# Routing groups of 8, 8, 8 and 12 tiles, evenly stepped, and two drains of GpSimd before the end, in an attention kernel with a top-1 mixture of experts

## The chip, the cores and the metric

One core of a Trainium2 chip runs the whole program. The time is device microseconds of one execution. The engines are named as in the profile: PE is TensorE (PEld its weight loads), DVE is VectorE, ACT is ScalarE, POOL is GpSimd, SP is SyncE, which here only issues transfers.

## The reference

For each of 8 batches and 8 heads, a 64 by 64 matrix kv is formed from k and v over 576 positions, q is multiplied by it, and the result is normed. The 4608 rows of 512 numbers then go through a mixture of 8 experts: each row goes to the expert with the greatest logit, alone.

```python
kv = np.einsum('bhsd,bhse->bhde', k, v)
out = np.einsum('bhsd,bhde->bhse', q, kv)
rms = np.sqrt(np.mean(out * out, axis=-1, keepdims=True) + 1e-06)
x = rows of (out / rms * g_norm)          # 4608 x 512

logits = x @ w_gate                        # 8 experts
e_idx = np.argmax(logits, axis=1)
gate_w = softmax(logits)[arange(N), e_idx]
eom = 1.0 / (1.0 + np.exp(-(x @ w_output_gate)))
for e in range(E):
    mask = e_idx == e
    h = np.maximum(x[mask] @ w1[e], 0.0)   # 512 -> 1024
    ye = h @ w2[e]                         # 1024 -> 512
    out[mask] = gate_w[mask, None] * eom[mask, e, None] * ye
```

## The kernel before

The kernel has two phases.

**Phase 1, attention and routing.** It goes through the 8 batches. For each, TensorE sums k and v into kv (`kvps`, L495), VectorE copies it (`kvc`, L503), and small matmuls make from it the matrix `aug`, which holds kv and its product with the gate's weights (`kvTps`, `mps`; `cps` at L477 is a filler that only keeps TensorE at work). Then the 36 tiles of 128 rows follow, 4.5 to a batch: `out_tile` multiplies q by `aug` (`ops`, L565), ScalarE copies the rows to `xrow` (L570), squares them (`sq`, L572) and copies the raw products with the gate's weights (`gp`, L573). One tile later VectorE sums the squares (`ss`, L586). Rows go to a table `xs` in memory in pieces of two tiles (`xs<-xrow`, L795, issued by SP), their scales in a second write per group (`xs<-xtail`, also L795).

The routing of the tiles is done in groups. `GR` gives their sizes, here 10, 10, 4 and 12 tiles. When the last tile of a group has its `ss`, a generator `route(gi)` starts for it, and after every further tile `advance` lets it go on to its next pause. How many tiles a pause lasts stands in a table, with 1 where nothing stands:

```python
WAITS = {(0, 2): 3, (1, 7): 2, (1, 2): 0, (1, 8): 2, (1, 5): 0, (0, 8): 2, (0, 6): 2}

def pause(k):
    for _ in range(WAITS.get((gi, k), 1)):
        yield 1
```

`route` computes on VectorE 1/rms (into `xtail`), scales the gate's products with it (`gp`, L642; for group 0 on GpSimd, for groups in `APART` in two halves, the gate's first), sums them to logits (`lg`, L646), finds the expert and writes a one-hot (`ohb`, L672). Matmuls on it (`rps`, L700 to L707) give each row its rank within its expert, `slots` and the remainder `lon`. Out of `lon` comes for each tile a 128 by 128 one-hot `la` (L743); `PLACES` says for each group which engine makes which: V is VectorE, P GpSimd, A ScalarE. With three VectorE operations `rrc` (L753 to L760) and `la`, TensorE sums a table of which row stands at which place of which expert (`tblps`, L773), from which VectorE makes the indices `gidx` and `oidx` of gathers and scatters.

The expert with most of the first 24 tiles is found at the end of the third group (`cnt` to `epos`); SP reads its number (`TENSOR_LOAD`) to choose the weights. Its first 384 rows form the lead run, which starts while the last 12 tiles are still being computed and routed. In both kernels the third group ends with tile 23.

**Phase 2, the experts.** There are nine runs: the lead run, the rest of that expert, and the seven others. Each run is gathered with one indirect DMA for each tile of 128 rows (`gather`, L244, on GpSimd's software queue), scaled by head with 1/rms (`scale_heads`, L252, GpSimd), transposed (`stage`) and multiplied with both weights (`mm1` L314 to `hps`, `mm2` L363 to `yps`). Weights come by SP (`wload`, L199) and are split in two parts (L219 to L229). ScalarE and VectorE scale the result (`y`, L373 or L371), and GpSimd scatters its rows to the output (L374). Run i+1 is gathered while run i is in its `mm1`.

In phase 1 the order is as the code is written, on every engine. In phase 2 it is written out by hand for TensorE, VectorE and ScalarE, and a scheduler sets it for GpSimd and SP. At the end stands a loop over rows that found no room in their expert's places (L1100; with these inputs it runs zero times), and the end of the program (L1168), where every engine drains and meets the others.

Of the kernel before, what the change touches and what calls it, by code (L numbers as in the profile page):

```python
# [21 lines left out]
P = 128  # L22
# [21 lines left out]

NOVER = NT + E

GR = (10, 10, 4, 12)
GROUPS = [list(range(sum(GR[:i]), sum(GR[:i+1]))) for i in range(len(GR))]
GMAX = max(GR)

LEAD_TILES = 24
LEAD_GROUP = [sum(GR[:i + 1]) for i in range(len(GR))].index(LEAD_TILES)
LEAD = LEAD_TILES * P // E // P * P

RUNS = [(0, 0, LEAD), (0, LEAD // P, CAP[0] - LEAD)] + [(p, 0, CAP[p]) for p in range(1, E)]
# [16 lines left out]
HOOKS = {15: 'R', 27: 'RR', 28: 'R', 31: 'RGW', 32: 'X', 34: 'NL'}  # L72
TAIL = "QLLLLRRRSLSRRSLLRRRLSLRRSRLSLL"

WAITS = {(0, 2): 3, (1, 7): 2, (1, 2): 0, (1, 8): 2, (1, 5): 0, (0, 8): 2, (0, 6): 2}

GPSIMD_GROUPS = 1
APART = (2,)


SPLITS = ['VV', 'AV', 'AV', 'AV', 'AV', 'AV', 'AV', 'AV']
NORMS = ("PPP", "VVVV")
PLACES = ['P', 'P', 'PAV', 'VAV']


COLD_B = 3
# [43 lines left out]
def tiles_of(i):  # L130

    _, t0, n = RUNS[i]
    return [(t0 + k, k * P, min(P, n - k * P)) for k in range(-(-n // P))]
# [6 lines left out]
def body(ctx: ExitStack, tc: tile.TileContext, kvm, rem, qT, wg, gn, w1, w2, kc, xs, tab, out):  # L140
    nc = tc.nc
# [39 lines left out]
    def give(t):  # L181
        free.append(held.pop(id(t))[0])
# [56 lines left out]
    def gather(i):  # L239
        p = RUNS[i][0]  # L240
        rows = xs[0:1 + LEAD_TILES * P] if i == 0 else xs
        for t, c0, M in tiles_of(i):
            x = take([P, XW], F32, "xg")
            nc.gpsimd.indirect_dma_start(  # L244
                out=x[:M, :], out_offset=None, in_=rows,
                in_offset=bass.IndirectOffsetOnAxis(ap=gidx[:M, p, t:t + 1], axis=0))
            xg[(p, t)] = x

    def scale_heads(x, eng):
        v = x[:, 0:DM].rearrange("p (h d) -> p h d", d=D)  # L250
# [88 lines left out]
    def mm2(i, k, events):  # L339
        nonlocal ny  # L340
        p = RUNS[i][0]
        t, c0, M = tiles_of(i)[k]
        C = RUNS[i][2]
        T = half(i)
        ps = ps_y.tile([P, DM], F32, name="yps", tag=f"y{ny % 2}")
        ny += 1
        tl = tails.pop((p, t))
        for f in range(8):
            h = h_of(i, f)
            wh, wl = wgt[(2, f // 2)]  # L350
            w0 = (f % 2) * DM
            w = [a[:, w0:w0 + DM] for a in (wh, wl)]
            if M == T:

                for b in (1, 0) if f == 0 else (0, 1):
                    rows = (1 + b) * P // 2
                    nc.tensor.matmul(ps[:rows], h[:, c0:c0 + rows], w[1 - b],  # L357
                                     start=(f == 0 and b == 1), stop=(f == 7 and b == 1))
            else:
                l0 = C - T + P if T else C  # L360
                hh, hl = h[:, c0:c0 + M], h[:, l0 + c0:l0 + c0 + M]
                for k, (a, b) in enumerate(((hh, w[0]), (hh, w[1]), (hl, w[0]))):
                    nc.tensor.matmul(ps[:M], a, b, start=(f == 0 and k == 0), stop=(f == 7 and k == 2))  # L363
            for e in events.get(f, ()):
                e()
        y = hp.tile([P, DM], F32, name="y", bufs=3)
        if M == T:
            y2 = hp.tile([P, DM], F32, name="y2")
            nc.scalar.copy(y2[:M], ps[P // 2:P // 2 + M])
            nc.vector.tensor_tensor(out=y[:M], in0=ps[:M], in1=y2[:M], op=ALU.add)  # L370
            nc.vector.tensor_scalar(out=y[:M], in0=y[:M], scalar1=tl[:M, 0:1], scalar2=None, op0=ALU.mult)  # L371
        else:
            nc.scalar.activation(y[:M], ps[:M], AF.Copy, scale=tl[:M, 0:1])  # L373
        i_ = nc.gpsimd.indirect_dma_start(  # L374
            out=out, out_offset=bass.IndirectOffsetOnAxis(ap=oidx[:M, p, t:t + 1], axis=0),
            in_=y[:M], in_offset=None, bounds_check=NTOK - 1, oob_is_err=False)
        tc.declare_no_dep(i_.ins, group="out", reason=nodep)
        tc.add_to_no_dep_group("out", i_.ins)


    def lead_run():
# [214 lines left out]
    def route(gi):  # L596
# [10 lines left out]
# [3 lines that stand above are left out]
# [27 lines left out]
        gpv = gp[:, :n]  # L637
        halves = [slice(0, E), slice(E, 2 * E)] if gi in APART else [slice(0, 2 * E)]

# [8 lines left out]
        scaled(halves[0], veng(gi))  # L648
        if gi in APART:
            scaled(halves[1], veng(gi))  # L650
# [81 lines left out]
        def low(ts_):  # L732
            for t in ts_:
                la = wk.tile([P, P], BF16, name="la", bufs=GMAX)
                las.append(la)
                e = PLACES[gi][t % len(PLACES[gi])]
                if e == "A":
# [300 lines left out]
    with tc.manual_schedule(engines={ET.PE, ET.Activation, ET.DVE}):  # L1038
        for i in range(len(RUNS)):
            p = RUNS[i][0]  # L1040
            T = len(tiles_of(i))
            last_run = i + 1 == len(RUNS)
            change = not last_run and RUNS[i + 1][0] != p
            if i == 0:
                gather(1)
                scale_rows(1)
                for _ in lead:
                    next(lead2, None)
                for _ in lead2:
                    pass  # L1050
            else:
                for f in range(8):
                    mm1(i, f)
                    if f % 2:
                        if i > 1:
                            split(p, 2, f // 2)
                        drop(1, f // 2)
                        if change:
                            wload(p + 1, 1, f // 2)
                    if f == 2 and not last_run:  # L1060
                        gather(i + 1)
                    if f == 3 and not last_run:
                        scale_rows(i + 1)
                    if i > 1:
                        next(listing, None)
            Tn = 0 if last_run else len(tiles_of(i + 1))

            at = {}

            def put(k, f, e, *a):  # L1070
                at.setdefault(k, {}).setdefault(f, []).append(lambda: e(*a))

            if change:
                for c in range(4):
                    at_ = (c, 0) if T >= 4 else divmod(c * T * 2, 8)
                    put(*at_, split, p + 1, 1, c)
                    put(*at_, wload, p + 1, 2, c)
            places = [(k, f) for k in range(T) for f in (2, 5)]
            places = places[-Tn:] if Tn > len(places) - 2 else places[:-1]
            for x in range(Tn):  # L1080
                put(*places[x * len(places) // Tn], stage, i + 1, x)
            order = list(range(T))
            if last_run and half(i):
                order.insert(1, order.pop())
            for k in order:
                mm2(i, k, at.get(k, {}))
            if i == 0:
                for h in hT[0]:
                    give(h)
            if i > 0:  # L1090
                for c in range(4):
                    drop(2, c)
# [105 lines left out]
```

## Time and profile before

| | us |
|---|---|
| time, median of 3 runs (lowest to highest) | 596.77 (596.24 to 603.41) |
| the profiled execution: its own time | 597.85 |
| its span | 596.0 |
| TensorE busy | 558.9 (94%) |
| VectorE busy | 255.3 (43%) |
| ScalarE busy | 223.7 (38%) |
| GpSimd busy | 149.4 (25%) |

The span goes from the first to the last instruction that the profiler saw. Times of rows count from its start. A row of a timeline has its start, its duration, engine, line, operation, what it writes and reads, and in brackets how long the engine had been idle before it and what it waited for. Lines and engines with a q at the end of the engine's name (POOLq, SPq) are those of its sequencer: drains, semaphores, DMA issues. The granted clock of TensorE is given as a share of its full 2.4 GHz.

### The profile page before, as it was taken

Reading aid. Unit: us, or ns where it says so; the run is one execution under the profiler, and the core shown is the slowest. Engines: PE = TensorE matmul, PEld = TensorE weight load, DVE = VectorE, ACT = ScalarE, POOL = GpSimd, SP = SyncE. Lnnn points to the kernel's source line nnn. Section 1 sums busy time; section 2 is a strip of 40 time slices with the busy share of each in tenths; the row PEclk is TensorE's granted clock in tenths of the full one; section 3 lists DMA queues with packets and bytes.
Section 4 is the critical chain, followed back from the end, with each engine's and each line's share of the span. In section 5 each row is a group of like instructions: output and inputs, shape, how many; then the busy total and the mean of one; then the engine's idle time right before and its main releaser. Section 6 shows DMA issues by size and latency. Waiting matters only on the chain.

```text
span 596.0 us, 10672 instructions
## 1 busy us (share of the span) xinstructions
PE 558.9 (94%) x4287; PEld 488.6 (82%) x4287; DVE 255.3 (43%) x555; ACT 223.7 (38%) x413; POOL 149.4 (25%) x154
## 2 busy tenths in 40 slices
PE   6999988858999999999999999999999999999991
PEld 4677867758797998899889987998798899889880
DVE  1125678697235555234432351344145334424300
ACT  1356646633135235223432342344235333423310
POOL 2001233402714502610360045006401620110010
PEclk9899979589999999999999999999999999999996
DMA  8999995862554523252334244324523352100000
GB/s 263 371 408 407 408 386 154 282 235 58 183 208 151 183 74 125 85 178 73 114 108 162 74 140 143 127 71 126 176 71 114 106 180 82 62 36 1 19 36 10
DMA packets 33460, 92.26 MB, mean 155 GB/s; under 512 B 8801, under 2 KB 8929, under 8 KB 33408
## 3 DMA queue, kind: packets, MB, share of 16 engines
q1 hardware_dynamic: 26672, 71.63, 34.2%
q0 software_dynamic: 6304, 19.70, 10.5%
q8 instruction: 35, 0.57, 0.4%
q10 hardware_dynamic: 432, 0.21, 0.1%
q14 instruction: 17, 0.14, 0.1%
HBM read 72.34 MB, written 19.70 MB: 154 GB/s over the span
## 4 chain that ended last, share of the span: by engine, by line
PE 65%; issue 17%; DMA 7%; DVE 4%; POOL 2%; ACT 2%; SPq 1%; POOLq 0%; DVEq 0%
PE yps L363 27%; PE hps L314 27%; PE kvps L495 3%; PE tps L276 2%; PE ops L565 2%; DMA ld<-qT 2%; PE yps L357 2%; POOL out L374 2%; DMA ld<-rem 2%; DMA ld<-kvm 2%; DMA wraw<-w 1%; PE cps L477 1%; DVE ss L586 1%; POOL xg L244 1%; DVE lg L646 1%
## 5 line engine op out<-in xcount | busy, mean ns | idle before, releaser
L314 PE MATMUL hps<-xT,whi 128*128 128x256 f32 (+8 forms) x1024 | 192.8, 306 | 4.8 <-DVE hT L330 4.4
L363 PE MATMUL yps<-whi,hT 128*128 128x512 f32 (+3 forms) x592 | 194.9, 397 | 0.0
L314 PEld LDWEIGHTS hps<-xT,whi 128*128 128x128 f32 x1024 | 160.1, 191 | 7.0 <-DVE hT L330 3.9
L363 PEld LDWEIGHTS yps<-whi,hT 128*128 128x128 f32 (+3 forms) x592 | 110.1, 186 | 24.0
L314 PE MATMUL hps<-xT,wlo 128*128 128x304 f32 (+8 forms) x512 | 119.5, 305 | 0.0
L363 PE MATMUL yps<-wlo,hT 128*128 128x512 f32 (+3 forms) x296 | 115.9, 392 | 0.0
L330 DVE SCALAR_TENSOR_TENSOR hT<-hps,hT 128x512 fp32r<-128x512 f32 (+6 forms) x112 | 58.0, 518 | 124.5 <-ACT hT L329 124.5
L329 ACT ACTIVATE hT<-hps 128x512 fp32r<-128x512 f32 (+6 forms) x112 | 51.6, 461 | 145.3 <-PE hps L314 115.5
L314 PEld LDWEIGHTS hps<-xT,wlo 128*128 128x128 f32 x512 | 87.3, 191 | 0.0
L244 POOL DMA_INDIRECT xg<-xs,gidx x42 | 42.8, 1019 | 168.8 <-PE tps L276 91.8
L374 POOL DMA_INDIRECT out<-y,oidx x42 | 44.5, 1060 | 155.0 <-ACT y L373 110.3
L363 PEld LDWEIGHTS yps<-wlo,hT 128*128 128x128 f32 (+3 forms) x296 | 55.1, 186 | 11.2
L222 DVE SCALAR_TENSOR_TENSOR wlo<-wraw,gcol,whi 128x1024 fp32r<-128x1024 f32 x32 | 44.0, 1375 | 40.3 <-ACT whi L219 40.3
L373 ACT ACTIVATE y<-yps,tl 128x512 f32<-128x512 f32 (+3 forms) x37 | 25.5, 689 | 71.4 <-PE yps L363 68.4
L252 POOL TENSOR_TENSOR xg<-xg 128x512 f32<-128x512 f32 (+7 forms) x39 | 41.6, 1069 | 33.9 <-DMA xg<-xs,gidx 32.9
L281 ACT CAST xT<-tps 128x512 fp32r<-128x512 f32 (+9 forms) x45 | 23.2, 518 | 69.1 <-PE tps L276 67.4
L282 DVE TENSOR_TENSOR xT<-tps,xT 128x512 fp32r<-128x512 f32 (+9 forms) x45 | 27.2, 605 | 45.6 <-ACT xT L281 45.1
L229 DVE TENSOR_TENSOR wlo<-wraw,whi 128x1024 fp32r<-128x1024 f32 x32 | 39.2, 1224 | 14.1 <-ACT whi L226 7.1
L565 PEld LDWEIGHTS ops<-aug,ld 64*128 64x128 f32 (+1 forms) x640 | 36.4, 190 | 7.3 <-ACT aug L527 3.2
L565 PE MATMUL ops<-aug,ld 64*128 64x80 f32 (+1 forms) x640 | 40.5, 283 | 1.7 <-ACT gp L573 0.7
L219 ACT ACTIVATE whi<-wraw,gcol 128x1024 fp32r<-128x1024 f32 x31 | 35.5, 1144 | 0.0
L226 ACT CAST whi<-wraw 128x1024 fp32r<-128x1024 f32 x32 | 33.2, 1040 | 1.4 <-DMA wraw<-w 1.4
(163 smaller groups left out, 398.9 us busy)
## 6 DMA issues: line engine op xcount, KB each, us to landing
wraw<-w SPq DMA_DIRECT2D x64, 512.0 KB, 3.5
ld<-kvm SPq DMA_DIRECT2D x32, 512.0 KB, 10.1
ld<-qT SPq DMA_DIRECT2D x18, 512.0 KB, 10.2
xs<-xrow SPq DMA_DIRECT2D x13, 512.0 KB, 11.6
xs<-xrow SPq DMA_DIRECT2D x2, 1280.0 KB, 14.6
ld<-rem SPq DMA_DIRECT2D x3, 512.0 KB, 10.2
xg<-xs,gidx POOLq DMA_INDIRECT x42, 3.5
out<-y,oidx POOLq DMA_INDIRECT x42, 3.0
```

Source lines behind the costliest of these rows:

```text
L219: he.activation(hi, r, AF.Copy, scale=gcol[:, 0:1])
L222: eng.scalar_tensor_tensor(out=lo, in0=r, scalar=gcol[:, 0:1], in1=hi.bitcast(F32), op0=ALU.mult, op1=ALU.subtract)
L226: he.copy(hi, r)
L229: eng.tensor_tensor(out=lo, in0=r, in1=hi.bitcast(F32), op=ALU.subtract)
L244: nc.gpsimd.indirect_dma_start(out=x[:M, :], out_offset=None, in_=rows, in_offset=bass.IndirectOffsetOnAxis(ap=gidx[:M, p, t:t + 1], axis=0))
L252: eng.tensor_tensor(out=v, in0=v, in1=f, op=ALU.mult)
L314: nc.tensor.matmul(ps[:, j, :n], w[:, o:o + P], x[d][:, j * N:j * N + n], start=(d == 0 and k == 0), stop=(d == 3 and k == 2))
L329: nc.scalar.activation(hh, x, AF.Relu)
L330: nc.vector.scalar_tensor_tensor(out=v(h[:, l:l + n]), in0=x, scalar=0.0, in1=hh.bitcast(F32), op0=ALU.max, op1=ALU.subtract)
L363: nc.tensor.matmul(ps[:M], a, b, start=(f == 0 and k == 0), stop=(f == 7 and k == 2))
L374: i_ = nc.gpsimd.indirect_dma_start(out=out, out_offset=bass.IndirectOffsetOnAxis(ap=oidx[:M, p, t:t + 1], axis=0), in_=y[:M], in_offset=N ...
L565: nc.tensor.matmul(ps[r0:r0 + m, u, p * W:(p + 1) * W], qt[g // 2][r, p, q0:q0 + m], augs[b % 3][r, p, :], start=True, stop=True)
```

## The change

The groups become 8, 8, 8 and 12 tiles. The table of pauses is empty, so each pause lasts one tile. The last group joins those whose logits are scaled and summed in two halves. In the third group VectorE makes six of the eight one-hots `la` and GpSimd two; before, of four, GpSimd made two and ScalarE and VectorE one each. A new function `settle` issues a drain on GpSimd that waits for a given DMA: once after the gather of the last run, once after the third scatter from the end. Lines behind it shift: the helpers of phase 2 by 8 (scales L260, scatters L382), phase 1 by 9 (`ss` L595, `la` L752, `tblps` L782, writes to `xs` L804), the loop to L1113, the end to L1181.

```diff
-GR = (10, 10, 4, 12)
+GR = (8, 8, 8, 12)
...
-WAITS = {(0, 2): 3, (1, 7): 2, (1, 2): 0, (1, 8): 2, (1, 5): 0, (0, 8): 2, (0, 6): 2}
+WAITS = {}
 
 GPSIMD_GROUPS = 1
-APART = (2,)
+APART = (2, 3)
...
-PLACES = ['P', 'P', 'PAV', 'VAV']
+PLACES = ['P', 'P', 'VVP', 'VAV']
...
         for t, c0, M in tiles_of(i):
             x = take([P, XW], F32, "xg")
-            nc.gpsimd.indirect_dma_start(
+            gathered = nc.gpsimd.indirect_dma_start(
...
+        return gathered
+
+    def settle(g_):
+
+        d_ = nc.gpsimd.drain()
+        tc.add_manual_dep(d_.ins, g_.ins.name,
+                          mybir.DependencyInfo(mybir.DependencyClass.Sync, mybir.DependencyReason.DATA),
+                          reason="order of GpSimd")
...
         tc.add_to_no_dep_group("out", i_.ins)
+        return i_
...
                     if f == 2 and not last_run:
-                        gather(i + 1)
+                        g_ = gather(i + 1)
+                        if i + 2 == len(RUNS):
+                            settle(g_)
...
             for k in order:
-                mm2(i, k, at.get(k, {}))
+                g_ = mm2(i, k, at.get(k, {}))
+                if last_run and k == order[-3]:
+                    settle(g_)
```

What stands in a row on the engines:

VectorE before, from the end of the third group's expert choice to its scales and the first use of the table (`eposf` and `epos` are the expert's number, `rdn` the softmax's sums, `ss` the sums of squares of tiles 24 and up):

```order
L902 TENSOR_REDUCE eposf<-t_124 128x1
L904 CAST epos<-eposf 128x1
L586 TENSOR_REDUCE ss<-sq 128x8
L753 TENSOR_TENSOR rrc<-cf,rhk 128x4x48
L755 TENSOR_REDUCE rdn<-rex 128x4
L757 TENSOR_TENSOR rrc<-rrc,gfull 128x4x48
L758 TENSOR_SCALAR rdn<-rdn 128x4
L760 TENSOR_SCALAR rrc<-rrc,cf 128x4x48
L761 TENSOR_SCALAR rdn<-rdn 128x4
L743 TENSOR_SCALAR la<-ni,rlon 128x128
L764 RECIPROCAL rdn<-rdn 128x2x4
L766 TENSOR_TENSOR xtail<-rdn 128x4
```

VectorE after, at the same place:

```order
L913 CAST epos<-eposf 128x1
L752 TENSOR_SCALAR la<-ni,rlon 128x128 x3
L595 TENSOR_REDUCE ss<-sq 128x8
L762 TENSOR_TENSOR rrc<-cf,rhk 128x8x48
L764 TENSOR_REDUCE rdn<-rex 128x8
L766 TENSOR_TENSOR rrc<-rrc,gfull 128x8x48
L767 TENSOR_SCALAR rdn<-rdn 128x8
L769 TENSOR_SCALAR rrc<-rrc,cf 128x8x48
L770 TENSOR_SCALAR rdn<-rdn 128x8
L752 TENSOR_SCALAR la<-ni,rlon 128x128 x3
L773 RECIPROCAL rdn<-rdn 128x2x8
L775 TENSOR_TENSOR xtail<-rdn 128x8
```

Six one-hots stand in the row in place of one, three of them ahead of a tile's `ss`, three ahead of the reciprocal; `rrc` and `rdn` are twice as wide.

TensorE before, where the first group's table is summed: the tile that two batches share (`ops` with two `aug`), and behind it the pairs of `la` and `tblps`, ten in all:

```order
L565 MATMUL ops<-aug_116,ld 64x80 x2
L565 MATMUL ops<-aug_117,ld 64x80 x2
L565 MATMUL ops<-aug_116,ld 64x80 x2
L565 MATMUL ops<-aug_117,ld 64x80 x2
L773 LDWEIGHTS la
L773 MATMUL tblps<-rrc,la 128x96
L773 LDWEIGHTS la
```

TensorE after, where the first group's table is summed (eight pairs of `la` and `tblps`, of which the first two stand here):

```order
L486 LDWEIGHTS ones
L486 MATMUL cps<-ones 128x512
L574 MATMUL ops<-aug_115,ld 128x80 x8
L782 LDWEIGHTS la
L782 MATMUL tblps<-rrc,la 128x96
L782 LDWEIGHTS la
L782 MATMUL tblps<-rrc,la 128x96
```

The first pair now stands behind the eight `ops` of the 17th tile, before behind the 23rd. The rank matmuls (`rps`) of the first group move from behind the 18th to behind the 15th tile, those of the second group from behind the 25th to behind the 23rd, its table from behind the 28th to behind the 26th. The third and the last group stay where they were (28th and 31st, 36th and 36th).

GpSimd after, in the stretch where the last run's rows are gathered and scaled, with the semaphores that an instruction waits for (DMASW are the landings of software DMAs, `ox`, `oy` don't occur here; a drain has no row of its own):

```order
L244 DMA xg<-xs,gidx 128x528 [waits DMAHW0_49,DMASW6_49,DVE_49]
L244 DMA xg<-xs,gidx 32x528 [waits DVE_49,DMASW7_49,PE_49,Pool_49]
L260 TENSOR_TENSOR xg<-xg 128x512 [waits DMASW6_49]
L382 DMA out<-y,oidx 4608x512 [waits DMASW0_49,Activation_49]
L260 TENSOR_TENSOR xg<-xg 32x512 [waits DMASW7_49]
L382 DMA out<-y,oidx 4608x512 [waits Activation_49]
L382 DMA out<-y,oidx 4608x512 [waits DMASW2_49,DVE_49]
```

The two gathers are the last ones; drain 1 stands between the scatter and the scale of the tile of 32 rows, and the wait for DMASW7, the last gather's landing, is the drain's as well. In the kernel before, the same rows stand in this order without it. Drain 2 stands between the third and the second scatter from the end. SP's order changes in one place: the read of the expert's number and the first `wraw<-w` now stand ahead of the third group's `xs<-xtail`, where they stood behind it; the writes of rows and scales before it follow the new group sizes (eight `xrow`, `xtail`, four `xrow`, `xtail`; before ten, `xtail`, two, `xtail`).

## Rows read from the trace of the kernel before

**Rows 1.** The page: busy time of each engine, share of the span, instructions.

```profile
PE 558.9 (94%) x4287; PEld 488.6 (82%) x4287; DVE 255.3 (43%) x555; ACT 223.7 (38%) x413; POOL 149.4 (25%) x154
```

**Rows 2.** Stretches: window, length, busy PE PEld DVE ACT POOL, clock, DMA share, GB/s.

```profile
82.00:89.00 7.00, 7.00 (x69) 5.24 (x70) 4.35 (x23) 3.22 (x10) 3.38 (x6) 0.50 1.06 382
...
150.00:484.00 334.00, 334.00 (x1941) 297.39 (x1941) 131.08 (x226) 117.64 (x182) 107.28 (x102) 1.00 0.40 129
...
583.00:596.00 13.00, 0.00 (x0) 0.00 (x0) 0.00 (x0) 0.42 (x1) 0.97 (x1) 0.61 0.04 12
```

**Rows 3.** The program's last line: durations ns (min/median/max), first to last start us.

```profile
L1168 POOLq DRAIN  x3: 46/103/7017, 588.1 to 595.7; - x3
...
L1168 PEldq DRAIN  x2: 8/8/8, 588.2 to 595.5; - x2
```

**Rows 4.** GpSimd's timeline over the last two runs: gather, scale, scatters.

```profile
473.02 0.88 POOL L244 DMA_INDIRECT xg<-xs,gidx  x1 [0.30 <-issue]
...
477.45 1.05 POOL L252 TENSOR_TENSOR xg<-xg 32x512 f32<-32x512 f32 x1
...
512.65 1.01 POOL L374 DMA_INDIRECT out<-y,oidx  x1 [28.64 <-ACT y L373]
...
572.82 0.97 POOL L374 DMA_INDIRECT out<-y,oidx  x1 [3.42 <-ACT y L373]
578.31 0.97 POOL L374 DMA_INDIRECT out<-y,oidx  x1 [4.52 <-ACT y L373]
583.70 0.97 POOL L374 DMA_INDIRECT out<-y,oidx  x1 [4.42 <-ACTq L1100]
```

**Rows 5.** DMA issues: count, KB each (where known), median us from issue to landing.

```profile
xg<-xs,gidx POOLq DMA_INDIRECT x42, 3.5
out<-y,oidx POOLq DMA_INDIRECT x42, 3.0
...
xs<-xtail SPq DMA_DIRECT2D x1, 32.0 KB, 2.2
```

**Rows 6.** GpSimd's timeline: one-hots of a group, and the lead run's first gather.

```profile
70.14 6.52 POOL L743 TENSOR_SCALAR la<-ni,rlon 128x128 bf16<-128x128 f32 x10 [15.33 <-DVE rlon L722]
...
103.50 1.08 POOL L244 DMA_INDIRECT xg<-xs,gidx  x1 [5.53 <-DVE ss L586]
```

**Rows 7.** VectorE's timeline: last batch's kv, and the third group to its scales.

```profile
92.92 0.42 DVE L503 COPY kvc<-kvps 128x256 f32<-128x256 f32 x1
...
94.18 0.41 DVE L646 TENSOR_REDUCE lg<-gp 128x32 f32<-128x256 f32 x1
...
98.85 0.35 DVE L753 TENSOR_TENSOR rrc<-cf,rhk 128x192 bf16<-128x192 f32 x1
...
99.73 0.28 DVE L743 TENSOR_SCALAR la<-ni,rlon 128x128 bf16<-128x128 f32 x1
99.92 0.19 DVE L764 RECIPROCAL rdn<-rdn 128x8 f32<-128x8 f32 x1
100.15 0.17 DVE L766 TENSOR_TENSOR xtail<-rdn 128x4 f32<-128x4 f32 x1
```

**Rows 8.** TensorE's timeline: two tiles, kv sums of two batches, the second group's ranks.

```profile
60.70 2.02 PE L565 MATMUL ops<-aug,ld 64*128 64x80 f32 x32
...
72.99 2.63 PE L495 MATMUL kvps<-ld 128*64 128x64 f32 x77
...
81.97 0.54 PE L705 MATMUL rps<-ohb,ones 128*128 128x80 bf16 x10 [2.47 <-DVE ohb L672]
...
88.76 3.71 PE L495 MATMUL kvps<-ld 128*64 128x64 f32 x80
```

**Rows 9.** ScalarE's timeline: the copy of tile 24's rows.

```profile
82.01 0.59 ACT L570 COPY xrow<-ops 128x512 f32<-128x512 f32 x1 [2.19 <-DMA xs<-xrow]
```

**Rows 10.** TensorE's timeline: the last group's ranks.

```profile
128.26 0.50 PE L705 MATMUL rps<-ohb,ones 128*128 128x96 bf16 x12 [2.95 <-DVE ohb L672]
```

**Rows 11.** VectorE's timeline: the last group's sum of logits.

```profile
125.01 1.74 DVE L646 TENSOR_REDUCE lg<-gp 128x192 f32<-128x1536 f32 x1
```

## The prediction

> **What bounds the kernel now.** I began with the busy times: TensorE is busy for 94% of the span [rows 1], so an edit pays only where TensorE stands still or runs at half clock, or before its first and after its last instruction. The stretches come next [rows 2]. From 150 us on TensorE works without a gap at full clock, so no engine beside it has anything to give there. From 82 to 89 us it is busy all the time, but the granted clock is 0.50, the lower level, 1.2 GHz. In the last 13 us of the span it does nothing, ScalarE 0.42 us and GpSimd 0.97 us of work. So there are two places to win: the routing, between about 58 and 130 us, where gather, weights and expert runs start, and the end.
>
> The end is read from the instructions on the program's last line [rows 3]. GpSimd's longest DRAIN begins at about 588.1 us and takes 7.017 us; its two others take 0.103 and 0.046 us, TensorE's 0.008 us. Nothing else runs while it lasts, and the remainder of the program follows within 0.9 us. The last scatter was issued at 583.70 [rows 4], and a scatter lands 3.0 us after its issue [rows 5]: at 586.7 all data is in memory. So the drain doesn't wait for data; it is 7 us of GpSimd's own time on the path that sets the end.
>
> **Drains.** What would make it long? The program has issued 42 gathers and 42 scatters through GpSimd's software queue [rows 5], and nothing had drained it. My reading is that a drain pays for each software DMA since the drain before it: 7.017 us / 84 = 0.084 us each. The two short drains right behind the long one, with nothing left to clear, speak for it; no row shows a drain after a known small number. In the changed order drain 1 stands behind 72 of the 84, drain 2 behind ten more, and the final drain behind the last two: 6.0, 0.84 and 0.17 us. The final one adds its floor of 0.1, so about 0.3 us in place of 7.0, **−6.7 us**.
>
> What the two new drains cost:
> - Drain 1 waits for the last gather, issued at 473.02 [rows 4] and landing 3.5 us later [rows 5], 476.5. It stands just ahead of the scale of the 32-row tile (477.45), so it would last from 477.4 to 483.4. Behind it wait this scale, two scatters, and whoever needs that tile. GpSimd has then a gap of 28.64 us until 512.65 [rows 4]. The 32-row tile is the fifth of the last run, wanted in the stages of the run that ends around 535; the two scatters hold two output buffers 6 us longer. TensorE's stretch has no waits there. I take 0.
> - Drain 2 waits for the landing of the scatter of 572.82 (3.0 us later, so until 575.8), then 0.84 us, to 576.7. The next scatter is at 578.31 and had waited 4.52 us for ScalarE [rows 4]. Covered by 1.6 us. It would begin to cost when a drain of ten takes more than 2.4 us.
>
> The Trainium skill speaks against this gain: "VectorE: DVE Perf Modes", section "The DRAIN you can't avoid", counts the drains of a program's end as boilerplate of a constant 12 ns or so on all engines. By that there is nothing to win at the end and the sum would be 596.6. Four of the five engines may agree with it, TensorE's row does (8 ns); GpSimd's 7,017 ns does not, and the measurement decides.
>
> **Routing, the lead gather.** The first gather is issued at 103.50 [rows 6]. It needs the third group's scales: xtail is computed at 100.15 [rows 7], the write lands 2.2 us after its issue [rows 5], so 102.5, and GpSimd issues about 1 us later. Since the copy of the last kv at 92.92 VectorE has had 7.23 us of work up to xtail. So gather = kvc + VectorE's stretch + about 3.3 us. The third group now has 8 tiles where it had 4, and its one-hots lie on VectorE (VVP):
> - five more one-hots: one takes 0.28 us and the next operation starts 0.19 us after it began, 0.235 as the mean [rows 7]: +1.2;
> - second half of the logits, 0.41 us for 4 tiles [rows 7], doubled less a fixed part as large as a small operation's: +0.27;
> - three rrc operations on twice the width, of which the first takes 0.35 us at 4 tiles [rows 7]: between nothing and that much again for the first, less for the two others; I take +0.4 together;
> - six small operations on twice the width: +0.2.
>
> That is +2.1 us. ScalarE loses a pair of operations there, which nobody waits for. SP now loads the expert's number and issues the first weight transfer ahead of this write; both need only epos, some 3.5 us older than xtail, so the write isn't late, and the weight comes earlier. Price 0.
>
> What is won against it is the start. VectorE's copy of the last kv (92.92) follows TensorE's batch of 80 at 88.76, which took 3.71 us at half clock, against 2.63 for 77 of them at full clock [rows 8]. Ahead of that, TensorE stood 2.47 us for the second group's one-hot before its rank matmuls (81.97), and the granted clock was 0.50 from 82 to 89 [rows 2]. In the new order the first group's table matmuls stand behind 17 tiles instead of 23, and the second group's rank matmuls behind 23 instead of 25, though this group now ends four tiles earlier: its one-hot has two tiles more to be ready, and the 2.47 us should go. Two things replace it. TensorE may now wait for GpSimd's one-hots, 0.65 us each by 6.52/10 [rows 6]. The first group's ranks would come at about 57.7, three tiles ahead of the end of the pair at 60.70 [rows 8], lon 1 us later; eight one-hots end at 63.9, and TensorE is behind the 17th tile, the first of that pair, at 61.7: 2.2 us. At the second group I take a little less. Both are hidden as long as ScalarE waits for the DMA in either kernel: its copy of tile 24 stood 2.19 us until the first row write landed, at 82.01 [rows 9], which no VectorE order moves. From there on TensorE had work until 92.5, 10.1 us at half clock; at full clock, by 2.63 to 3.71, it would be some 7.4: kvc at 90.1, or 92.5 if the clock falls as before. VectorE, busy 4.35 of those 7 us [rows 2], I take to be ready by then. So kvc is won by 0.4 to 2.8 us, and the gather comes between −0.7 and +1.7 us: I take **+0.5**, the middle, since the row that decides (the clock) can go both ways.
>
> **Routing, the last group.** It is ranked at 128.26, after 2.95 us of TensorE waiting for the one-hot [rows 10]. Ahead of it VectorE has the sum of all logits, 1.74 us [rows 11]; with APART the gate half alone, about 0.93, so the one-hot comes 0.8 earlier, less 0.1 for the product cut in two. **−0.7**, all of it TensorE's. The second half then lies behind the one-hot, where VectorE's wait is not TensorE's.
>
> **Sum.** Against the profiled execution, 597.85 us (span 596.0 and 1.85 around it): −6.7 + 0 + 0.5 − 0.7 = −6.9, so 590.9. The median of the runs is 596.77, 1.1 below the profiled one; by it 589.9, rounded **590.0**. Bounds by the same rows: −0.7 and +1.7 at the gather give 588.7 and 591.1; if the two waits for GpSimd's one-hots are not hidden either (up to 2.2), 593.3; if the last group gains nothing, 594.0.
>
> **Rivals.**
> 1. *A drain's price is fixed*, 7 us whatever is outstanding. For it: a single long row can't tell a count from a constant. Against it: the two short ones. Then the final drain remains at 7.0, drain 1 is still hidden in the 28.64 us gap, and drain 2 runs from 575.8 to 582.8: the scatters of 578.31 and 583.70 go at 582.9 and 584.0, 0.3 to 0.6 us late, all of it on the end. No gain: 596.8 + 0.6 − 0.2 = 597.2, slower than before. It decides from 6.5 us per drain upwards. 0.10.
> 2. *The first drain pays a start-up*, and later ones don't, whatever was issued. The rows don't speak against it, since the long drain is the first of the three and the next take 0.1 us and less. Drain 1 would take the 7 us in GpSimd's gap, the final drain 0.1: −6.9 in place of −6.7, 589.7 in all. The time is the forecast's, the drains' lengths are not. 0.12. The Trainium skill has such a rule, "GPSIMD Engine Reference", section "2.1 Instruction dispatch": the first call of freshly loaded code costs about 6 us (5.95), with no instruction of its own in the profile. By its figure 7.0 − 5.95 = 1.1 us, an estimate, would be left at the end, and the sum would be 590.7.
> 3. *The routing loses*: the clock falls as before, VectorE's +2.1 us is not paid back and TensorE waits for GpSimd's one-hots in addition: +3 at the gather, 596.8 − 6.7 + 3 − 0.7 = 592.4. For it: GpSimd's 6.5 us groups are the slowest thing in this stage. 0.10.
> 4. *The routing wins*: without the 2.47 us stop the clock stays full through 82 to 91, and the lead run's half-clock stretches shrink as well. For it: the batch takes 2.63 in place of 3.71 us at full clock, and there are several such steps. 2 us at the gather: 596.8 − 6.7 − 2 − 0.7 = 587.4. 0.10.
>
> **How the numbers follow.** The forecast has 0.58, its own range 588.5 to 592. The range over all takes in rivals 2, 3 and 4 and the bounds, 586.5 to 595.0, and leaves rival 1 and the tails out, 0.15 or so. A difference under 2%, 11.9 us, can't be told from none. Within it lie the forecast and all rivals: same 0.95; faster by over 2% would take both ends of the routing gain and more, 0.03; slower 0.02.
>
> **What would show it.** In the profile of the changed kernel: GpSimd's DRAIN on the program's last line at about 0.3 us (7.0: rival 1), and two new ones, 6 us at 477 and 0.8 us at 576 (7 and 0.1: rival 2), with no idle TensorE after 150 us. The first gather between 102.8 and 105.2. No wait for the one-hot before the second group's rank matmuls, and a granted clock from 82 to 89 above 0.50 (if not, rival 3). The last group's ranks at about 127.5. I am wrong if the final drain stays long with two DMAs behind the last one, or if the time TensorE wins in the routing is not the gather's.

## The result, and the profile after

The changed kernel takes 591.40 us (median of four runs, 589.36 to 591.65 but for one run of 1433 us, which is left out of the comparison; 591.15 without it), against 596.78 us. The ratio is 0.9897, 95% interval 0.986 to 0.9933: about 6 us faster, clear of the noise and under the 2% line. The forecast was 590.0, range 586.5 to 595.0. The profiled execution took 591.15 us, 6.70 less than the one before; its span is 589.4 us.

The end first, from the instructions on the program's last line (durations in ns, min/median/max) of the changed kernel, and the two new drains, which carry the line of `settle`:

```profile
L1181 POOLq DRAIN  x3: 46/176/204, 587.8 to 589.1; - x3
L252 POOLq DRAIN  x1: 7659/7659/7659, 476.5 to 476.5; - x1
L252 POOLq DRAIN  x1: 866/866/866, 575.9 to 575.9; - x1
```

The long one among the final drains [rows 3] has gone from 7.017 to 0.204 us, and the two new ones stand where the text said. GpSimd's timeline of the changed kernel around them:

```profile
477.07 1.03 POOL L382 DMA_INDIRECT out<-y,oidx  x1 [0.15 <-issue]
484.25 1.03 POOL L260 TENSOR_TENSOR xg<-xg 32x512 f32<-32x512 f32 x1 [6.15 <-issue]
...
513.02 1.01 POOL L382 DMA_INDIRECT out<-y,oidx  x1 [25.29 <-ACT y L381]
...
573.19 0.97 POOL L382 DMA_INDIRECT out<-y,oidx  x1 [3.42 <-ACT y L381]
578.68 0.97 POOL L382 DMA_INDIRECT out<-y,oidx  x1 [4.52 <-ACT y L381]
584.07 0.97 POOL L382 DMA_INDIRECT out<-y,oidx  x1 [4.42 <-ACTq L1113]
```

Drain 1's record begins at 476.48, while GpSimd still has the scatter of 477.07 ahead of it, which ends at 478.10. From there to the drain's end at 484.14 are 6.04 us, and it is 6.04 in every kernel below that has this drain behind as many DMAs (nine profiles with this one); the scale of the 32-row tile comes 6.8 us later than in [rows 4]. Nobody misses it: GpSimd's gap is 25.29 us instead of 28.64, and the next scatter waits for ScalarE as before. Drain 2 ends at 576.80, and the scatter of 578.68 has waited 4.52 us for ScalarE, to the hundredth what it waited before.

The last scatter is issued at 584.07, 0.37 us later than before; from there to the end of the span it is 5.3 us instead of 12.3. So the end gave 7.0, and all that lies ahead of it took 0.37 back.

The stretches of the changed kernel (window, length, busy time of PE, PEld, DVE, ACT, POOL, granted clock, DMA share, GB/s), and TensorE's timeline through the routing:

```profile
82.00:89.00 7.00, 6.15 (x97) 4.67 (x98) 6.86 (x24) 4.21 (x13) 4.44 (x8) 0.93 1.09 352
...
150.00:484.00 334.00, 334.00 (x1940) 297.10 (x1940) 132.01 (x226) 117.52 (x181) 104.53 (x99) 1.00 0.40 129
```

```profile
61.70 0.22 PE L782 MATMUL tblps<-rrc,la 128*128 128x96 bf16 x1 [0.36 <-POOL la L752]
...
63.43 0.22 PE L782 MATMUL tblps<-rrc,la 128*128 128x96 bf16 x1 [0.36 <-POOL la L752]
63.58 1.51 PE L574 MATMUL ops<-aug,ld 64*128 64x80 f32 x16
65.01 3.83 PE L504 MATMUL kvps<-ld 128*64 128x64 f32 x80
...
78.79 0.35 PE L714 MATMUL rps<-ohb,ones 128*128 128x64 bf16 x8
...
86.49 0.22 PE L782 MATMUL tblps<-rrc,la 128*128 128x96 bf16 x1 [0.42 <-POOL la L752]
86.64 1.12 PE L574 MATMUL ops<-aug,ld 64*128 64x80 f32 x16
87.69 4.21 PE L504 MATMUL kvps<-ld 128*64 128x64 f32 x80
...
128.74 0.70 PE L714 MATMUL rps<-ohb,ones 128*128 128x96 bf16 x12 [1.43 <-DVE ohb L681]
```

The wait of 2.47 us before the second group's ranks [rows 8] is gone (78.79 has none), and the clock from 82 to 89 us is 0.93 instead of 0.50. In their place TensorE waits for one `la` after the other in the first group's table (six waits, 2.2 us with those of the second), and the batch of 87.69 falls into a half-clock stretch of its own: 4.21 us, longer than the 3.71 of before. The last kv and the third group on VectorE, and the first gather on GpSimd:

```profile
92.35 0.42 DVE L512 COPY kvc<-kvps 128x256 f32<-128x256 f32 x1 [2.11 <-ACT aug L510]
...
98.15 0.67 DVE L752 TENSOR_SCALAR la<-ni,rlon 128x128 bf16<-128x128 f32 x3
...
100.57 0.67 DVE L752 TENSOR_SCALAR la<-ni,rlon 128x128 bf16<-128x128 f32 x3
...
101.43 0.17 DVE L775 TENSOR_TENSOR xtail<-rdn 128x8 f32<-128x8 f32 x1
...
126.30 0.94 DVE L655 TENSOR_REDUCE lg<-gp 128x96 f32<-128x768 f32 x1
```

```profile
104.81 1.08 POOL L244 DMA_INDIRECT xg<-xs,gidx  x1 [6.95 <-DVE ss L595]
```

The kv comes 0.57 us earlier, xtail 1.28 us later, the gather 1.31 us later than in [rows 6] and [rows 7]. The last group's sum is 0.94 us where it was 1.74 [rows 11], and its ranks come 23.9 us behind the gather instead of 24.8.

### The profile page after: what moved, and what is told of

Its sections match the earlier page's. It is cut to its first block, busy times and chain, and to the rows that moved or that the text cites. A ratio compares the mean times of both kernels' runs of the same rounds, so it can differ in the third digit from the quotient of the medians.

```text
span 589.4 us, 10666 instructions
## 1 busy us (share of the span) xinstructions
PE 562.4 (95%) x4287; PEld 491.6 (83%) x4287; DVE 258.3 (44%) x562; ACT 223.2 (38%) x411; POOL 145.8 (25%) x150
## 4 chain that ended last, share of the span: by engine, by line
PE 79%; DMA 7%; issue 5%; DVE 4%; POOL 2%; ACT 1%; POOLq 0%; SPq 0%; DVEq 0%
PE hps L322 35%; PE yps L371 33%; PE yps L365 3%; PE tps L284 3%; DMA ld<-qT 2%; PE ops L574 2%; DMA ld<-rem 2%; PE kvps L504 2%; POOL la L752 2%; DMA ld<-kvm 2%; DMA xg<-xs,gidx 1%; DVE ss L595 1%; DMA out<-y,oidx 0%; DVE wlo L222 0%; DVE wlo L229 0%
## 5 line engine op out<-in xcount | busy, mean ns | idle before, releaser
L382 POOL DMA_INDIRECT out<-y,oidx x42 | 44.5, 1059 | 147.9 <-ACT y L381 106.6
L260 POOL TENSOR_TENSOR xg<-xg 128x512 f32<-128x512 f32 (+7 forms) x39 | 41.7, 1072 | 41.0 <-DMA xg<-xs,gidx 33.9
L574 PE MATMUL ops<-aug,ld 64*128 64x80 f32 (+1 forms) x640 | 41.8, 289 | 0.6 <-issue 0.6
## 6 DMA issues: line engine op xcount, KB each, us to landing
xs<-xrow SPq DMA_DIRECT2D x13, 512.0 KB, 11.6
```

The source lines that it names most:

```text
L260: eng.tensor_tensor(out=v, in0=v, in1=f, op=ALU.mult)
L382: i_ = nc.gpsimd.indirect_dma_start(out=out, out_offset=bass.IndirectOffsetOnAxis(ap=oidx[:M, p, t:t + 1], axis=0), in_=y[:M], in_offset=N ...
L574: nc.tensor.matmul(ps[r0:r0 + m, u, p * W:(p + 1) * W], qt[g // 2][r, p, q0:q0 + m], augs[b % 3][r, p, :], start=True, stop=True)
```

## The experiments

Twelve runs follow: ten other kernels, one of them twice, and the changed one again. In the table "kv", "gather" and "last scatter" are starts in the profiled execution of each: the last `kvc` copy, the first gather, the last scatter.

**Is it the drains, or the routing?** Two kernels, each with one half of the change. The drains alone (against the changed kernel):

```diff
-GR = (8, 8, 8, 12)
-WAITS = {}
-APART = (2, 3)
-PLACES = ['P', 'P', 'VVP', 'VAV']
+GR = (10, 10, 4, 12)
+WAITS = {(0, 2): 3, (1, 7): 2, (1, 2): 0, (1, 8): 2, (1, 5): 0, (0, 8): 2, (0, 6): 2}
+APART = (2,)
+PLACES = ['P', 'P', 'PAV', 'VAV']
```

> The kernel before with the two drains alone; groups, pauses, halves and one-hots as before. My theory (a drain pays about 0.083 us for each software DMA since the drain before): drain 1 takes about 6.0 us, drain 2 about 0.85, the final one about 0.2 in place of 7.0, and the first gather stays at 103.5: 596.8 - 6.9 = 589.9, a little less than the changed kernel, whose last scatter stands 0.37 us later than before. Rival (the time came from the routing): 596 to 597, and the final drain stays near 7.

And the routing alone:

```diff
                         g_ = gather(i + 1)
-                        if i + 2 == len(RUNS):
-                            settle(g_)
...
                 g_ = mm2(i, k, at.get(k, {}))
-                if last_run and k == order[-3]:
-                    settle(g_)
```

> The changed kernel without its two drains. My theory: the final drain is back at 7.0 us, and the routing alone costs what the last scatter of the changed kernel is late, 0.4 us: 597.1. The forecast's routing term would give 596.6; rival (the routing is what gained): below 594.

Measured: the drains alone 589.07 us against 596.95 of before on the same chip, ratio 0.9875 (0.9853 to 0.9896); the routing alone 597.01, ratio 1.0002 (0.9982 to 1.0023). The final drains of the two:

```profile
L1181 POOLq DRAIN  x3: 46/103/204, 587.7 to 588.5; - x3
```

```profile
L1177 POOLq DRAIN  x3: 46/103/7017, 585.0 to 592.9; - x3
```

The whole gain is the drains'. Without them the final one is 7,017 ns again, to the nanosecond that of [rows 3], although everything ahead of it stands otherwise. The routing is worth nothing within 1.4 us either way; the loss of 0.4 us read off one profile is too small for these runs to tell.

**What does a drain pay for?** One long drain can't tell a count from a time, a number of rows or a constant. The counts below are of DMAs in GpSimd's software queue. The kernel before issues 85 of them, one more than the prediction's 84: 42 gathers, 42 scatters and, at its start, a plain write of 2.1 KB.

```profile
1.60 0.76 POOL L416 DMA_DIRECT2D xs<-xtail  x1 [0.32 <-POOL xtail L414]
```

In one kernel a drain stands behind the gather of every run and behind every scatter of the last run:

```diff
                         g_ = gather(i + 1)
-                        if i + 2 == len(RUNS):
-                            settle(g_)
+                        settle(g_)
...
-                if last_run and k == order[-3]:
+                if last_run:
                     settle(g_)
```

> The changed kernel with a drain after the gather of every run and after every scatter of the last run, so that known numbers of software DMAs lie between drains: 15, 8, 9, 11, 10, 10, 10, 8 and then 1, 1, 1. My theory: 1.24, 0.66, 0.75, 0.91, 0.83, 0.83, 0.83, 0.66 us and about 0.1 to 0.15 for each single one, the one of 32 rows like those of 128. Rival by rows moved (0.72 ns a row): the drain behind the 32-row scatter is 0.07 us shorter than those behind 128 rows. Rival by a fixed price: each 7 us, and the run is longer by tens of us. The time is that of the changed kernel within 1 us.

Its drains, one by one in order of time:

```profile
L252 POOLq DRAIN  x1: 1299/1299/1299, 165.9 to 165.9; - x1
L252 POOLq DRAIN  x1: 696/696/696, 205.6 to 205.6; - x1
L252 POOLq DRAIN  x1: 772/772/772, 251.2 to 251.2; - x1
...
L252 POOLq DRAIN  x1: 697/697/697, 565.5 to 565.5; - x1
L252 POOLq DRAIN  x1: 119/119/119, 570.3 to 570.3; - x1
L252 POOLq DRAIN  x1: 113/113/113, 574.6 to 574.6; - x1
```

15 DMAs 1.299 us, 8 DMAs 0.696, 9 DMAs 0.772, 8 again 0.697, a single one 0.11 to 0.12. The drain of 570.3 stands behind the scatter of 32 rows, that of 574.6 behind one of 128: 119 and 113 ns, so rows don't count. The last two, not printed, took 113 and 117 ns behind one scatter each.

The four at 307.0, 363.8, 419.5 and 475.0 have 10 or 11 DMAs to clear and do not show the price. The last of them, with the scatter ahead of it and the scale behind it:

```profile
475.55 1.03 POOL L382 DMA_INDIRECT out<-y,oidx  x1 [0.16 <-issue]
L252 POOLq DRAIN  x1: 4002/4002/4002, 475.0 to 475.0; - x1
479.07 1.04 POOL L260 TENSOR_TENSOR xg<-xg 32x512 f32<-32x512 f32 x1 [2.49 <-issue]
```

Read as drain 1 was, from the end of that scatter, the four take 2.2 to 3.3 us, where 0.83 and 0.91 were expected. In each the scatter had not landed when GpSimd was done with issuing it, and the drain ends 0.4 to 0.5 us after it lands (2.8 to 3.9 us behind the start of its issue). So the price by the count is shown for drains whose DMAs have landed, and for drain 1, which has 73 to clear and ends well after its scatter's landing. That a drain also waits for what is in flight is read from these four; no run tests it by itself.

The time was 589.96 us, in the one run made: ten drains more than the changed kernel has cost nothing that shows.

The other kernel goes the other way: no drain of its own, but more to clear. The kernel before, with a second gather of 8 rows behind the gather of every tile, from the third run on:

```diff
             xg[(p, t)] = x
+            if i > 1:
+                w = mem.tile([8, XW], F32, name="again", tag="again", bufs=1)
+                nc.gpsimd.indirect_dma_start(
+                    out=w, out_offset=None, in_=rows,
+                    in_offset=bass.IndirectOffsetOnAxis(ap=gidx[:8, p, t:t + 1], axis=0))
```

> The kernel before, without any drain of its own, with 36 more gathers of 8 rows each into a tile that nobody reads: 121 software DMAs in place of 85, but only 3% more rows. My theory (count): the final drain takes 121 x 0.0826 = 10.0 us, and the time is 3 us longer if GpSimd's extra issues stay hidden. Rival by rows: 7.2 us. Rival fixed: 7.0 us.

The instructions of its last lines:

```profile
L1173 POOLq DRAIN  x3: 46/103/9957, 608.5 to 619.0; - x3
```

9.957 us for 121 DMAs where 10.0 was forecast: (9,957 − 7,017) / 36 = 81.7 ns for each further one, whether of 8 rows or of 128. With 85, 121, 15, 8 and 1 the price is 0.08 us a DMA and 0.03 to 0.07 us besides. The time itself was a miss: 621.12 us in the one run made, not 3 us more, since the extra gathers did not stay hidden. TensorE waits for the lateness that they bring, 10.5 us for `hT` and 5.9 for `y` (before 4.4 and none), and around the two longest of these waits, from 250 to 290 us, its granted clock is 0.79, where it was 1.00 before:

```profile
PE hps L319 <- DVE hT L335: 10.5, 4, 6.2
PE yps L362 <- ACT y L378: 5.9, 1, 5.9
250.00:290.00 40.00, 27.90 (x138) 24.56 (x137) 7.97 (x15) 6.39 (x10) 24.57 (x25) 0.79 0.40 124
```

The waits are about 12 us more than before, the lower clock costs some 5 to 8 us (an estimate from the 0.79 over 40 us, part of which is waiting), and the drain 2.9: most of the 24 us. The forecast had taken GpSimd's free time for free places in its order. The length of the drain is not touched by that.

**Which of the two drains?** The changed kernel without drain 1, and without drain 2:

```diff
-                        if i + 2 == len(RUNS):
-                            settle(g_)
```

> The changed kernel without drain 1. My theory: the drain near the end now clears 83 software DMAs and takes 6.9 us, from about 576 to 583; the scatter of 578.7 waits for it until 583, the last one hardly, and the final drain is 0.2 again: the time is that of the changed kernel plus 0.1 to 0.4 us. Rival (a single drain so near the end costs what it saves): 596.

```diff
-                if last_run and k == order[-3]:
-                    settle(g_)
```

> The changed kernel without drain 2. My theory: the final drain clears 12 software DMAs and takes 1.0 us in place of 0.2: 0.8 us longer than the changed kernel. Rival (the drain near the end is what counts): the final one is 7.

Measured: 591.38 us (0.9924, 0.9899 to 0.995) with the late drain alone, 590.86 (0.9907, 0.9883 to 0.9931) with the early one alone; the changed kernel has 0.9897. In the first the drain takes 6.851 us for 83 DMAs, and GpSimd comes to the last two scatters late:

```profile
571.15 0.97 POOL L382 DMA_INDIRECT out<-y,oidx  x1 [3.42 <-ACT y L381]
581.61 0.97 POOL L382 DMA_INDIRECT out<-y,oidx  x1 [9.48 <-issue]
582.88 0.97 POOL L382 DMA_INDIRECT out<-y,oidx  x1 [0.31 <-POOLq L1111]
```

By the spacing of all other kernels but the one with extra gathers (10.88 us from this scatter to the last) the last one would go at 582.03; it goes at 582.88, 0.85 us late, where I had expected 0.1 to 0.4. In the second the final drain takes 1.032 us for the 12 DMAs since drain 1 (1.0 expected). So either drain alone does most of it. Each has nearly the same left to pay, 0.85 us at the last scatter or 0.83 us in the final drain. The times can't tell them apart, nor what the second drain adds from nothing.

**The routing, term by term.** Four kernels undo one part each; three of these ran beside the changed kernel on one chip. The changed kernel without the last group's halves:

```diff
-APART = (2, 3)
+APART = (2,)
```

> The changed kernel with the last group's logits scaled and summed whole again, as before. My theory: the halves are what shortens the way from the first gather to the last scatter (480.2 us in the kernel before and with the drains alone, 477.8 to 479.3 in all kernels with halves); without them it is 480.2 again, and the time is 1 to 1.5 us above the changed kernel. Rival (the earlier first weight of the lead run, which the new order of SP brings, does it): 478.6 still.

With the third group's one-hots dealt out as before:

```diff
-PLACES = ['P', 'P', 'VVP', 'VAV']
+PLACES = ['P', 'P', 'PAV', 'VAV']
```

> The changed kernel with the third group's eight one-hots dealt to GpSimd, ScalarE and VectorE as before, so that VectorE makes two instead of six. My theory: VectorE's stretch from the last kv to the first gather, 12.46 us in all kernels with the new groups, shrinks by 4 x 0.22 to about 11.6, and the gather comes 0.9 us earlier for the same kv. Rival (ScalarE's three pairs or GpSimd's three one-hots become the late ones, and TensorE's table and the indices come after xtail's landing): 12.46 or more.

With the first two groups' one-hots shared by VectorE and GpSimd:

```diff
-PLACES = ['P', 'P', 'VVP', 'VAV']
+PLACES = ['VP', 'VP', 'VVP', 'VAV']
```

> The changed kernel, with every second one-hot of the first two groups made by VectorE instead of GpSimd. My theory: TensorE's waits for GpSimd's one-hots in the table matmuls (2.2 us in the changed kernel) go, the batch behind them runs at full clock more often, the last kv is copied at about 90 instead of 92.35, and the first gather comes near 102.5: about 1 us faster than the changed kernel, 589 to 590. Rival (those waits are hidden, as I forecast): the last kv at 91 to 92.4 and the same time as the changed kernel.

The drains and the halves, with the old groups, pauses and places, run on two chips:

```diff
-GR = (8, 8, 8, 12)
-WAITS = {}
-PLACES = ['P', 'P', 'VVP', 'VAV']
+GR = (10, 10, 4, 12)
+WAITS = {(0, 2): 3, (1, 7): 2, (1, 2): 0, (1, 8): 2, (1, 5): 0, (0, 8): 2, (0, 6): 2}
+PLACES = ['P', 'P', 'PAV', 'VAV']
```

> The two drains and the last group's logits in halves; groups, pauses and the third group's one-hots as before. My theory: the first gather stays at 103.3, as with the drains alone, and from there to the last scatter it takes 0.7 us or a little more less (479.5 or less in place of 480.2), because the last group's one-hot comes earlier: 588.3. Rival (what the changed kernel wins behind the gather comes from the lead run and its weights, not from the halves): 480.2 as before, 589.1.

> The two drains and the halves with the old groups, beside the changed kernel on the same chip. My theory: the old groups have a first gather 1 us earlier (kv later by 0.7, VectorE's stretch 1.7 shorter) and all that the drains and the halves give: 1 us faster than the changed kernel. Rival (the groups cost nothing): no difference.

And the changed kernel again, on the chip of the last one:

> The changed kernel itself, beside the next one on the same chip. 589.5 to 591.5; from the first gather to the last scatter 478.6 to 479.3, from the last kv to the first gather 12.46.

| kernel | ratio to before (95%) | kv | gather | kv to gather | gather to last scatter |
|---|---|---|---|---|---|
| before | 1 | 92.92 | 103.50 | 10.58 | 480.20 |
| drains alone | 0.9875 (0.9853 to 0.9896) | 92.34 | 103.29 | 10.95 | 480.19 |
| drains, halves | 0.9866 (0.9845 to 0.9887) | 90.74 | 101.51 | 10.77 | 478.50 |
| the same again | 0.9861 (0.9844 to 0.9878) | 91.66 | 102.31 | 10.65 | 478.31 |
| changed | 0.9897 (0.986 to 0.9933) | 92.35 | 104.81 | 12.46 | 479.26 |
| changed again | 0.9903 (0.9884 to 0.9922) | 92.51 | 104.97 | 12.46 | 479.54 |
| routing alone | 1.0002 (0.9982 to 1.0023) | 89.98 | 102.45 | 12.47 | 478.61 |
| shared one-hots | 0.9900 (0.9879 to 0.9921) | 91.60 | 104.07 | 12.47 | 477.77 |
| no halves | 0.9897 (0.9877 to 0.9917) | 90.72 | 103.17 | 12.45 | 479.30 |
| third group PAV | 0.9882 (0.9862 to 0.9902) | 91.62 | 103.19 | 11.57 | 479.46 |

Four things follow.

*The way from kv to gather* is the steadiest number of the whole study: 12.45 to 12.47 us in every kernel with the new groups and VVP, 10.58 to 10.95 with the old. So a group of 8 with six one-hots on VectorE costs 1.7 us there. With PAV it is 11.57, where 11.6 was expected; ScalarE and GpSimd don't come late. What is left of the 1.7 us, 0.8, goes with the wider group and the one one-hot that VectorE has more than before even so.

*kv itself goes with the clock.* The stretch from 58 to 93 us, in the changed kernel and with the routing alone:

```profile
58.00:93.00 35.00, 31.71 (x557) 26.37 (x554) 24.39 (x79) 18.29 (x50) 10.04 (x16) 0.90 1.05 386
58.00:93.00 35.00, 31.55 (x589) 26.56 (x583) 25.90 (x84) 19.50 (x50) 9.40 (x15) 0.95 1.04 384
```

With the new groups kv comes at 89.98 to 90.80 where this clock is 0.95 (three profiles), at 91.47 to 92.51 where it is 0.90 (the other six). With the old groups it comes at 91.66 to 92.92 at 0.85 and at 90.74 in the one profile at 0.90. So one profile can't price the routing. The gather of the drains with halves, too, came at 101.51 and 102.31, where 103.3 was expected, mostly because kv came 1.6 and 0.7 us earlier than with the drains alone.

*Taking away the waits for GpSimd's one-hots wins nothing.* With the one-hots shared, TensorE's first table has none:

```profile
61.27 0.57 PE L782 MATMUL tblps<-rrc,la 128*128 128x96 bf16 x8
61.77 1.12 PE L574 MATMUL ops<-aug,ld 64*128 64x80 f32 x16
```

Yet kv comes at 91.60, inside the spread of the new groups (89.98 to 92.51), and the ratio is 0.9900 beside 0.9897 and 0.9903. The theory behind this kernel, that the waits cost 1 us, fell. The forecast's own word, hidden, agrees with it; it is not shown alone, since VectorE here makes the one-hots that GpSimd no longer does.

*The halves bring the one-hot earlier, but no time that can be measured with the new groups.* From gather to the last group's ranks it takes 24.8 and 24.6 us without them in the old order and 24.9 in the new one, 23.5 to 24.3 in all kernels with them: in the means 0.6 us with the old groups and 0.9 with the new. To the last scatter, though, the kernel without halves needs 479.30, not the 480.2 I expected, and its time of 589.93 us is no longer than the changed kernel's 590.51. With the old groups the same halves go with 1.8 us less to the last scatter, by time 0.5 to 0.8 us, within the intervals. Why the two orders answer differently stays open.

**A better version.** The drains and the halves with the old groups took 587.34 to 588.44 us where the changed kernel, on the same chip, took 589.50 to 592.07: 587.95 against 590.51, no run of the one in the range of the other. It beats both kernels; the new groups, with their pauses and places, are the part to leave out. The kernel with PAV, on this chip too, lies between (589.55), within the intervals. The expectation said 1 us, the medians say 2.6, and the profiles of the pair show it at the gather (102.31 against 104.97; the changed kernel took 479.54 from there to the last scatter, a little above the 478.6 to 479.3 expected). Not all of it is the groups': over the profiles the old order's gather comes at 101.51 to 103.50, the new one's at 102.45 to 104.97, 1.2 us apart in the mean (four profiles, without the kernel with extra gathers, and the eight with VVP, of which the table leaves out those of the kernels with one drain and with a drain for each run).

## Why the prediction held

- **The drains** were right in mechanism and size. Forecast 6.0, 0.84 and 0.3 us, measured 6.04, 0.866 and 0.204; −6.7 at the end, measured −7.0 from the last scatter to the end of the span. That a drain pays by the number of software DMAs since the one before, 0.084 us each, was an inference from one row; drains behind 1, 8, 9, 15, 83, 85 and 121 DMAs now show it, at 0.082; what GpSimd does for each of them no run shows. The count itself was one short: 85 and not 84. That a drain may also wait for a DMA in flight the text did not ask; drain 1 had one ahead of it and was long enough to hide that. That both new ones are covered is shown by the scatter of 578.68, which waited 4.52 us for ScalarE with and without a drain ahead of it.
- **Rival 1** (fixed price) is refuted by 113 ns behind one DMA, **rival 2** (a start-up, paid once) by drain 2's 0.866 and the final 0.204 behind a first drain of 6.04; rival 1's sum, 597.2, also lies 6 us off the time, but rival 2's, 589.7, does not, so only the lengths could tell there. The Trainium skill's rule of a first call of 6 us ("GPSIMD Engine Reference", section "2.1 Instruction dispatch") does not describe this drain: with 121 DMAs it took 9.957 us.
- **The drains as boilerplate of 12 ns on all engines** (the Trainium skill, "VectorE: DVE Perf Modes", section "The DRAIN you can't avoid") holds for the other four engines here, 7 to 17 ns, and not for GpSimd, whose drains on the program's last line took 40 to 251 ns with nothing to clear and up to 9,957 ns by what it had issued.
- **The lead gather**, forecast at +0.5 (−0.7 to +1.7): +1.31 in the profiled pair, +1.2 in the mean over all profiles. Its two halves were both mis-sized. VectorE's longer way was put at +2.1 and is +1.7. The win at kv was put at 0.4 to 2.8 us, middle 1.6, and is 0.57 in the pair and 0.6 in the mean. The step that gave too much is "kvc at 90.1 if the clock stays full": where it does stay full through 82 to 93 us (the kernels without halves, with PAV, and those with one drain) kv still comes at 90.7 to 91.6, and a half-clock stretch lies earlier there, between 62 and 70 us. No profile is without one. TensorE's waits for GpSimd's one-hots, put at 2.2 us and a little less, are 1.4 and 0.8. Rival 3 (+3 at the gather) and rival 4 (−2) both lie off the +1.3 measured.
- **The clock** could go both ways, as the text said: in kernels with the same routing the half-clock stretch lies now around 65 us, now around 88, and the batch ahead of the last kv takes from 2.70 to 4.21 us.
- **The last group**, forecast −0.7: 0.6 to 0.9 us at its ranks, counted from the gather. The ranks themselves come at 128.74, not at the 127.5 that the text gave as a sign: that figure left out the gather's lateness. As time the term isn't shown, since the kernel without halves is no slower than the changed one. The routing's sum of −0.2 agrees with 1.0002 (0.9982 to 1.0023), but an interval of over 1 us either way can't bear out a sum whose gather term was 0.7 us too low.
- **The total** came 1.4 us above the forecast, of which the gather's 0.8, read from profiles, may be a part; all of it is within the runs' own spread.

## What to carry to other kernels

A busy engine isn't always working on your program's data: before tuning the middle, look at what runs after the last useful instruction, and ask what it is proportional to. A cost that grows with the number of things outstanding can be paid in instalments, wherever the engine has a gap longer than the instalment; here one early drain in a gap of 28 us was worth 6 us, and a second one hardly anything. By the four rows of 307 to 475 us an instalment is best placed where no DMA is in flight ahead of it, or where it outlasts the landing. Where several edits come in one change, time them apart: beside the drains the regrouping cost 1.3 us (against the drains alone, intervals overlapping) to 2.6 us (against the old groups with halves, on one chip), and the drains hid it.

## What was not expected

The instruction that GpSimd runs ahead of the final loop follows the same count. It took 1.899 us in the kernel before; with 121 software DMAs it takes

```profile
L1105 POOLq INC_SWDGE_SEM  x1: 2620/2620/2620, 604.5 to 604.5; - x1
```

and 0.233 us in the changed kernel, 0.439 with drain 1 alone: about 0.02 us for each DMA since the last drain. In the kernel before it ends at 586.25, ahead of the last scatter's landing (issued at 583.70, 3.0 us), and so sets no time there.

GpSimd had 317 us of idle time between 150 and 583 us in the kernel before (433 less 107.3 and 8.6 busy), and 36 small gathers still cost over 20 us. They share one buffer, so each waits for the one ahead to land, and what stands behind them in GpSimd's order waits with them (45.7 us in 25 waits); where they stood there was no room for that.
